# Token-factor normalisations of six operations at other places of a mixture-of-experts kernel on one core

## The chip, the cores and the metric

One Trainium2 chip, one of its cores. The metric is the device time of one execution in microseconds (us). Shown are the median of three runs and one execution that the profiler recorded. The engines are called as the profile calls them: PE is TensorE, DVE is VectorE, ACT is ScalarE, POOL is GpSimd, SP issues the DMAs.

## The reference, cut to what matters

The program runs an mLSTM attention, a dense feed-forward layer, and a mixture of eight experts whose token factors are normalised over rows and columns eight times. Only the last part bears on the change:

```python
logits = x @ w_gate                        # x: 1536 x 320, w_gate: 320 x 8
logits = logits - logits.max()
P = np.exp(logits)
for _ in range(8):
    P /= P.sum(1, keepdims=True) + 1e-09   # rows: over the 8 experts
    P /= P.sum(0, keepdims=True) + 1e-09   # columns: over the 1536 tokens
    P *= N / E
for e in range(E):                         # F = 1024
    ye = np.maximum(x @ w1[e], 0.0) @ w2[e]
    out += P[:, e:e + 1] * ye
```

## The kernel before

All products are made of fp32r matmuls on values split into a high and a low part. After attention and the dense layer comes `tc.manual_schedule()`: from there each engine works through its instructions in the order in which the Python code emits them, and the order is written by hand.

The work of the experts is cut into units of 256 hidden columns: four units for each of eight experts, `experts[0]` to `experts[31]`, and two halves of 768 tokens, `q` = 0 and 1. `order` lists the 64 pairs: units 0, 1, 2 for q = 0, then the same for q = 1, then unit 3 for both, then one unit after the other for both halves. For the i-th pair, `up_c(i)` computes the hidden values by seven products of four matmuls each (`product`, lines 835 to 838), accumulated in four PSUM banks `b0` to `b3`: a fast matrix multiplication, which needs seven sums of pieces of the input (`X`, in 7 slices of 3 parts) and of the weights. Around them ACT copies the first product to `s0`; DVE adds it into `s1`, `s2` and into `c11`, `c10`, `c01` (lines 863, 866, 854), which frees banks 3, 2 and 3 again; ACT makes `hh` (rounded, line 855) and a full-precision copy (856) of each, POOL the low part `hl` (857). `hh00` and `hl00` come straight from bank 0 by ACT and DVE (872, 873). `down_c(i)` computes six outputs `y` of 128 tokens, six matmuls each (lines 172 to 174), in three PSUM banks in turn: the fourth output needs the bank of the first, so it needs the first to have been taken out. For the first unit (n = 0) an output is copied into `acc` (by ACT if it is odd, line 902, by DVE if it is even, line 904), for the others it is added by DVE (906 or 908). The loop calls `up_c(i + 1)`, then `down_c(i)`.

Everything else is hung into slots: `when(g, slot, fn)` has `fn` emitted at slot 0 to 6 behind the seven products of `up_c(g + 1)`, or at slot 7 to 12 behind the six outputs of `down_c(g)`. What is called **group g** here is that stretch, `up_c(g + 1)` and `down_c(g)`; group -1 is `up_c(0)`. Each function issues to several engines at once, and on each its instructions stand behind what was emitted there before. In the slots are:

- for q = 1, three positions (each two blocks of 128 tokens) that become `X[1]`: `repeat` (POOL copies), `turn` (4 PE transposes into the one bank of pool `ps_s`, and an ACT copy `rawE` or `rawx`, line 251), `sums` (two DVE subtractions for each k, line 257), `high` (an ACT conversion of 4 or 3 slices, line 222), `low` (DVE, 225), `rest` (POOL, 229);
- the gate: `logits` (matmuls, line 757), `logits_turn` to `exps`, which find the maximum and the exponentials `Pg`, 128 x 12 x 8; then eight times `rows` (798 to 801), `columns` (a matmul by ones into `cps`, 805) and `columns_end` (808 to 811);
- `scale_first` (918), which scales the accumulators of expert 0 by `Pg` before those of expert 1 are added;
- loading, `sums`, `split1` and `split2` of the next units' weights (ACT 213 and 222; POOL 214, 201, 225, 229).

Of the kernel before, what the change touches and what calls it, by code (L numbers as in the profile page):

```python
# [38 lines left out]
def mlstm_moe_kernel(ctx, tc, qp, q3, kp, kn, vn, gates_in, og, cst_in, scr_in, w_in, w_out, w_gate, w1, w2, out):  # L39
# [703 lines left out]
    nc.gpsimd.memset(ones, 1.0)  # L743
    Pg = cp.tile([P, NCK, E], F32, tag="Pg", name="Pg")
# [44 lines left out]
    def top_all():  # L789
        gate_state['mps'] = ps_s.tile([P, 512], F32, tag="b1", name="mps2")  # L790
        nc.tensor.matmul(gate_state['mps'][:, 0:1], ones[0:1, :], gate_state['m1'][:, 0:1], start=True, stop=True)
# [5 lines left out]
    def rows():  # L797
        nc.vector.tensor_reduce(out=rs, in_=Pg, axis=AX.X, op=ALU.add)
        nc.vector.tensor_scalar(out=rs, in0=rs, scalar1=1e-9, scalar2=None, op0=ALU.add)
# [3 lines left out]
    def columns(it):  # L803
        gate_state['cps'] = ps_s.tile([P, NCK, E], F32, tag="b1", name=f"cps{it}")
        nc.tensor.matmul(gate_state['cps'], ones, Pg, start=True, stop=True)

    def columns_end():
        nc.vector.tensor_reduce(out=cs, in_=gate_state['cps'].rearrange("p t e -> p e t"), axis=AX.X, op=ALU.add)
        nc.vector.tensor_scalar(out=cs, in0=cs, scalar1=1e-9, scalar2=None, op0=ALU.add)
        nc.vector.reciprocal(cs, cs)  # L810
        nc.vector.scalar_tensor_tensor(out=Pg, in0=Pg, scalar=float(NT / E), in1=cs.unsqueeze(1).to_broadcast([P, NCK, E]),
                                       op0=ALU.mult, op1=ALU.mult)
# [72 lines left out]
    def down_c(i):  # L885
# [6 lines left out]
        for b in range(2):  # L892
            for p in range(HP):
# [7 lines left out]
                if n == 0 and t % 2:  # L901
                    nc.scalar.activation(o, y, AF.Copy)
                elif n == 0:
                    nc.vector.tensor_copy(o, y)  # L904
# [27 lines left out]
    for g, s, p, k in ((-1, 2, 1, 0), (-1, 4, 1, 1), (0, 0, 2, 0), (0, 3, 2, 1)):  # L932
        when(g, s, x1[p].turn, k, ps_s, rawE if p == 1 else None)
    for p, times in enumerate((((-1, 0), (-1, 1), (-1, 3), (-1, 4)), ((0, 1), (0, 2), (0, 4), (0, 5)), ((0, 8), (0, 9), (0, 11), (1, 0)))):
        for k in range(2):
            if p:
                when(*((-1, 5), (-1, 6), (0, 6), (0, 7))[2 * p - 2 + k], x1[p].sums, V, k)
            when(*times[k], x1[p].high, k)
            when(*times[2 + k], x1[p].low, k, V)
            when(*times[2 + k], x1[p].rest, k, GP)  # L940

    for g, s, q, i in ((1, 4, 0, 0), (1, 7, 0, 1), (1, 9, 1, 0), (1, 12, 1, 1)):
# [146 lines left out]
```

## Time and profile before

| | |
|---|---|
| median of 3 runs | 983.21 us (982.13 to 984.79) |
| the profiled execution | 981.5 us, its span 979.8 us |
| PE busy | 944.1 us, 96% of the span |
| DVE, ACT, POOL busy | 60%, 51%, 62% |
| mean granted clock of PE | 0.974 |

The experts take the span from 296 us on. In the timelines a row gives the start, the duration, engine and line, output and input tiles, shapes and the number of merged instructions; brackets at the end hold the engine's idle time before it and what released it. PE's matmuls are pipelined, so successive rows overlap: what counts is the distance of their starts. In the view of stretches the granted clock is a share of full speed: 1.00 is 2.4 GHz, 0.50 is 1.2 GHz.

### The profile page before, as it was taken

Reading aid. Unit: us, or ns where it says so; the run is one execution under the profiler, and the core shown is the slowest. Engines: PE = TensorE matmul, PEld = TensorE weight load, DVE = VectorE, ACT = ScalarE, POOL = GpSimd, SP = SyncE. Lnnn points to the kernel's source line nnn. Section 1 sums busy time; section 2 is a strip of 40 time slices with the busy share of each in tenths; the row PEclk is TensorE's granted clock in tenths of the full one; section 3 lists DMA queues with packets and bytes.
Section 4 is the critical chain, followed back from the end, with each engine's and each line's share of the span. In section 5 each row is a group of like instructions: output and inputs, shape, how many; then the busy total and the mean of one; then the engine's idle time right before and its main releaser. Section 6 shows DMA issues by size and latency. Waiting matters only on the chain.

```text
span 979.8 us, 16868 instructions
## 1 busy us (share of the span) xinstructions
PE 944.1 (96%) x6174; PEld 918.3 (94%) x6174; DVE 583.5 (60%) x1137; ACT 496.0 (51%) x969; POOL 606.2 (62%) x615
## 2 busy tenths in 40 slices
PE   7699999999998988999999999999999999999998
PEld 5588998999997888999999999999999999999998
DVE  5977524152566568666666656666566665666655
ACT  5757544534656343654554545445454454544542
POOL 3552634533475455577677777777777777777762
PEclk7779999999999999999999999999999999999999
DMA  7644321011110100111111111111111111111102
GB/s 254 205 156 134 107 72 60 29 53 39 30 56 21 36 19 28 33 50 49 36 36 43 49 50 36 36 44 49 49 36 36 44 49 49 36 36 44 41 1 81
DMA packets 57160, 56.63 MB, mean 58 GB/s; under 512 B 7558, under 2 KB 47670, under 8 KB 57078
## 3 DMA queue, kind: packets, MB, share of 16 engines
q1 hardware_dynamic: 57078, 55.56, 18.7%
q8 instruction: 48, 0.79, 0.3%
q14 instruction: 34, 0.28, 0.1%
HBM read 53.57 MB, written 1.97 MB: 57 GB/s over the span
## 4 chain that ended last, share of the span: by engine, by line
PE 85%; DVE 7%; ACT 3%; issue 2%; POOL 1%; DMA 1%; SPq 1%; DVEq 0%; ACTq 0%; POOLq 0%
PE y L172 11%; PE y L173 11%; PE y L174 11%; PE b L835 8%; PE b L838 8%; PE b L836 8%; PE b L837 7%; PE ha L165 7%; PE ya L172 2%; PE ya L174 2%; PE ya L173 2%; PE yps L471 2%; PE sps L457 1%; PE zps L475 1%; DVE c L854 1%
## 5 line engine op out<-in xcount | busy, mean ns | idle before, releaser
L857 POOL TENSOR_TENSOR hl<-c,hh 128x384 fp32r<-128x384 f32 x192 | 196.8, 1025 | 185.2 <-ACT c L856 160.1
L172 PE MATMUL y<-w_e,hh 128*128 128x320 f32 x768 | 237.7, 310 | 3.0 <-DVE acc L904 1.7
L173 PE MATMUL y<-w_e,hh 128*128 128x320 f32 x768 | 236.3, 308 | 0.0
L174 PE MATMUL y<-w_e,hl 128*128 128x320 f32 x768 | 236.0, 307 | 0.0
L908 DVE SCALAR_TENSOR_TENSOR acc<-y,Pg,acc 128x320 f32<-128x320 f32 x336 | 179.4, 548 | 63.3 <-PE y L174 56.1
L855 ACT ACTIVATE hh<-c 128x384 fp32r<-128x384 f32 x192 | 99.9, 520 | 218.0 <-DVE c L854 218.0
L835 PE MATMUL b<-X,w_e 128*128 128x384 f32 x448 | 152.9, 341 | 1.4 <-DVE c L854 1.4
L836 PE MATMUL b<-X,w_e 128*128 128x384 f32 x448 | 151.6, 338 | 0.0
L838 PE MATMUL b<-X,w_e 96*128 96x384 f32 x448 | 151.5, 338 | 0.0
L837 PE MATMUL b<-X,w_e 128*128 128x384 f32 x448 | 151.0, 337 | 0.0
L172 PEld LDWEIGHTS y<-w_e,hh 128*128 128x128 f32 x768 | 144.1, 188 | 4.8 <-DVE acc L904 2.4
L173 PEld LDWEIGHTS y<-w_e,hh 128*128 128x128 f32 x768 | 144.0, 188 | 0.0
L174 PEld LDWEIGHTS y<-w_e,hl 128*128 128x128 f32 x768 | 144.0, 187 | 0.0
L544 POOL TENSOR_TENSOR hla<-gg,hha 128x256 fp32r<-128x256 f32 x90 | 72.6, 810 | 95.9 <-ACT hha L543 84.4
L165 PE MATMUL ha<-xT,w_a 128*128 128x256 f32 x768 | 111.1, 288 | 0.9 <-ACT xT L282 0.6
L856 ACT ACTIVATE c<-c 128x384 f32<-128x384 f32 x192 | 100.9, 525 | 17.8 <-ACT hh L855 0.7
L854 DVE TENSOR_TENSOR c<-b,s 128x384 f32<-128x384 f32 x192 | 100.8, 552 | 11.8 <-PE b L838 4.5
L165 PEld LDWEIGHTS ha<-xT,w_a 128*128 128x128 f32 x768 | 101.9, 193 | 5.3 <-issue 2.2
L873 DVE SCALAR_TENSOR_TENSOR hl<-b,hh 128x384 fp32r<-128x384 f32 x64 | 35.7, 558 | 102.2 <-ACT hh L872 102.2
L201 POOL TENSOR_TENSOR raw_e<-raw_e 128x256 f32<-128x256 f32 x116 | 84.4, 738 | 4.5
L835 PEld LDWEIGHTS b<-X,w_e 128*128 128x128 f32 x448 | 85.0, 190 | 2.2 <-DVE c L854 1.7
L836 PEld LDWEIGHTS b<-X,w_e 128*128 128x128 f32 x448 | 85.2, 190 | 0.0
(164 smaller groups left out, 1547.6 us busy)
## 6 DMA issues: line engine op xcount, KB each, us to landing
raw_e<-in_w_dram SPq DMA_DIRECT2D x32, 320.0 KB, 2.9
raw_e<-in_w_dram SPq DMA_DIRECT2D x62, 128.0 KB, 2.2
raw_e<-in_w_dram SPq DMA_DIRECT2D x248, 32.0 KB, 1.8
raw_a<-in_w_in_dram SPq DMA_DIRECT2D x8, 768.0 KB, 4.3
raw_a<-in_w_out_dram SPq DMA_DIRECT2D x8, 640.0 KB, 3.9
R<-in_kp_dram SPq DMA_DIRECT2D x11, 256.0 KB, 2.9
R<-in_qp_dram SPq DMA_DIRECT2D x11, 256.0 KB, 3.0
R<-in_vn_dram SPq DMA_DIRECT2D x11, 184.5 KB, 2.5
```

The costliest lines, as they stand in the source:

```text
L165: nc.tensor.matmul(h_ps, t1[:, ws, c * P:(c + 1) * P], xt[:, xs, t0:t0 + n], start=(j == 0), stop=(j == len(MM1) - 1),)
L172: nc.tensor.matmul(y_ps, a, t2[:, c, :], start=first, stop=False)
L173: nc.tensor.matmul(y_ps, a, t2[:, 2 + c, :], start=False, stop=False)
L174: nc.tensor.matmul(y_ps, b, t2[:, c, :], start=False, stop=last)
L835: nc.tensor.matmul(bank, f[:, 0], b[:, 0], start=fresh, stop=False, skip_group_check=not fresh)
L836: nc.tensor.matmul(bank, f[:, 0], b[:, 2], start=False, stop=False, skip_group_check=not fresh)
L837: nc.tensor.matmul(bank, f[:, 2], b[:, 0], start=False, stop=False, skip_group_check=not fresh)
L838: nc.tensor.matmul(bank, f[0:K3, 1], b[0:K3, 1], start=False, stop=True, skip_group_check=not fresh)
L854: nc.vector.tensor_tensor(c, part, plus, op=ALU.add)
L856: nc.scalar.activation(c, c, AF.Relu)
L857: nc.gpsimd.tensor_tensor(hl[a][b], c, hh[a][b].bitcast(F32), op=ALU.subtract)
L908: nc.vector.scalar_tensor_tensor(out=o, in0=y, scalar=Pg[:, 2 * HP * q + t, e:e + 1], in1=o, op0=ALU.mult, op1=ALU.add)
```

## The change

- `Pg` becomes a view of a tile `Pgx` of 13 x 9: a ninth column and a thirteenth block hold constants (1e-9, and 1e-9 / 128), so that the row sums and the column sums already contain the 1e-9. The factor N / E goes into the ones of the column matmul, by E / N. `rows` and `columns_end` have three DVE operations each instead of four.
- All six outputs of the first unit are copied by ACT.
- Slots: the sums of position 1 for q = 1 stand one and four slots later, its `high`, `low`, `rest` some four slots later; position 2's `turn` one and two slots later, its sums three, its conversions in group 1. The conversion `split2` of unit 1 goes from group -1 to group 0. The logits of q = 1 go from group 1 to group 2, the gate's steps follow into groups 2 and 3. `columns` stay at slots 2 and 8, the first at slot 8 of group 3 instead of slot 2; `columns_end` now stands at slots 3 and 9 (before 4 and 10), `rows` at 3 and 11 (before 4 and 10). `scale_first` comes one group later.

```diff
@@ -740,8 +740,14 @@
     ps_u = ctx.enter_context(tc.tile_pool(name="ps_u", bufs=1, space=PSUM))
 
     ones = cp.tile([P, P], F32, tag="ones", name="ones")
-    nc.gpsimd.memset(ones, 1.0)
-    Pg = cp.tile([P, NCK, E], F32, tag="Pg", name="Pg")
+    nc.gpsimd.memset(ones, float(E / NT))
+    one = cp.tile([1, P], F32, tag="one", name="one")
+    nc.gpsimd.memset(one, 1.0)
+
+    Pgx = cp.tile([P, NCK + 1, E + 1], F32, tag="Pg", name="Pg")
+    nc.gpsimd.memset(Pgx[:, 0:NCK], 1e-9)
+    nc.gpsimd.memset(Pgx[:, NCK], 1e-9 / P)
+    Pg = Pgx[:, 0:NCK, 0:E]
     rs = cp.tile([P, NCK], F32, tag="rs", name="rs")
     cs = cp.tile([P, E], F32, tag="cs", name="cs")
     nmx = cp.tile([P, 1], F32, tag="nmx", name="nmx")
@@ -788,28 +794,26 @@
 
     def top_all():
         gate_state['mps'] = ps_s.tile([P, 512], F32, tag="b1", name="mps2")
-        nc.tensor.matmul(gate_state['mps'][:, 0:1], ones[0:1, :], gate_state['m1'][:, 0:1], start=True, stop=True)
+        nc.tensor.matmul(gate_state['mps'][:, 0:1], one, gate_state['m1'][:, 0:1], start=True, stop=True)
 
     def exps():
         nc.vector.tensor_copy(nmx, gate_state['mps'][:, 0:1])
         nc.scalar.activation(Pg, Pg, AF.Exp, bias=nmx)
 
     def rows():
-        nc.vector.tensor_reduce(out=rs, in_=Pg, axis=AX.X, op=ALU.add)
-        nc.vector.tensor_scalar(out=rs, in0=rs, scalar1=1e-9, scalar2=None, op0=ALU.add)
+        nc.vector.tensor_reduce(out=rs, in_=Pgx[:, 0:NCK], axis=AX.X, op=ALU.add)
         nc.vector.reciprocal(rs, rs)
         nc.vector.tensor_tensor(Pg, Pg, rs.unsqueeze(2).to_broadcast([P, NCK, E]), op=ALU.mult)
 
     def columns(it):
-        gate_state['cps'] = ps_s.tile([P, NCK, E], F32, tag="b1", name=f"cps{it}")
-        nc.tensor.matmul(gate_state['cps'], ones, Pg, start=True, stop=True)
+        gate_state['cps'] = ps_s.tile([P, NCK + 1, E], F32, tag="b1", name=f"cps{it}")
+        nc.tensor.matmul(gate_state['cps'], ones, Pgx[:, :, 0:E], start=True, stop=True)
 
     def columns_end():
+
         nc.vector.tensor_reduce(out=cs, in_=gate_state['cps'].rearrange("p t e -> p e t"), axis=AX.X, op=ALU.add)
-        nc.vector.tensor_scalar(out=cs, in0=cs, scalar1=1e-9, scalar2=None, op0=ALU.add)
         nc.vector.reciprocal(cs, cs)
-        nc.vector.scalar_tensor_tensor(out=Pg, in0=Pg, scalar=float(NT / E), in1=cs.unsqueeze(1).to_broadcast([P, NCK, E]),
-                                       op0=ALU.mult, op1=ALU.mult)
+        nc.vector.tensor_tensor(Pg, Pg, cs.unsqueeze(1).to_broadcast([P, NCK, E]), op=ALU.mult)
 
 
 
@@ -898,10 +902,8 @@
                 for a in range(2):
                     mm2(y, hh[a][b], hl[a][b], p, u.w2, a, a == 0, a == 1)
                 o = acc[q][:, t]
-                if n == 0 and t % 2:
+                if n == 0:
                     nc.scalar.activation(o, y, AF.Copy)
-                elif n == 0:
-                    nc.vector.tensor_copy(o, y)
                 elif e == 0:
                     nc.vector.tensor_tensor(o, y, o, op=ALU.add)
                 else:
@@ -929,31 +931,35 @@
 
     for p in (1, 2):
         when(-1, (0, 2)[p - 1], x1[p].repeat, copy_rest)
-    for g, s, p, k in ((-1, 2, 1, 0), (-1, 4, 1, 1), (0, 0, 2, 0), (0, 3, 2, 1)):
+    for g, s, p, k in ((-1, 2, 1, 0), (-1, 4, 1, 1), (0, 1, 2, 0), (0, 5, 2, 1)):
         when(g, s, x1[p].turn, k, ps_s, rawE if p == 1 else None)
-    for p, times in enumerate((((-1, 0), (-1, 1), (-1, 3), (-1, 4)), ((0, 1), (0, 2), (0, 4), (0, 5)), ((0, 8), (0, 9), (0, 11), (1, 0)))):
+
+    for p, sums, highs, lows, rests in ((0, None, ((-1, 0), (-1, 1)), ((-1, 3), (-1, 4)), ((-1, 3), (-1, 4))),
+                                        (1, ((-1, 6), (0, 3)), ((0, 5), (0, 6)), ((0, 7), (0, 8)), ((0, 7), (0, 9))),
+                                        (2, ((0, 9), (0, 10)), ((1, 4), (1, 5)), ((1, 8), (1, 10)), ((1, 6), (1, 8)))):
         for k in range(2):
             if p:
-                when(*((-1, 5), (-1, 6), (0, 6), (0, 7))[2 * p - 2 + k], x1[p].sums, V, k)
-            when(*times[k], x1[p].high, k)
-            when(*times[2 + k], x1[p].low, k, V)
-            when(*times[2 + k], x1[p].rest, k, GP)
-
-    for g, s, q, i in ((1, 4, 0, 0), (1, 7, 0, 1), (1, 9, 1, 0), (1, 12, 1, 1)):
+                when(*sums[k], x1[p].sums, V, k)
+            when(*highs[k], x1[p].high, k)
+            when(*lows[k], x1[p].low, k, V)
+            when(*rests[k], x1[p].rest, k, GP)
+
+    for g, s, q, i in ((1, 4, 0, 0), (1, 7, 0, 1), (2, 1, 1, 0), (2, 5, 1, 1)):
         when(g, s, logits, q, i)
-    for s, fn in ((0, logits_turn), (2, logits_sum), (4, top_turn), (6, top_one), (8, top_all), (9, exps), (11, rows)):
-        when(2, s, fn)
+    for g, s, fn in ((2, 8, logits_turn), (2, 9, logits_sum), (2, 11, top_turn), (2, 12, top_one), (3, 1, top_all), (3, 2, exps),
+                     (3, 7, rows)):
+        when(g, s, fn)
+
     for it in range(8):
-        g, s = 3 + it // 2, 6 * (it % 2)
-        when(g, s + 2, columns, it)
-        when(g, s + 4, columns_end)
-        if it < 7:
-            when(g, s + 4, rows)
+        g = 3 + (it + 1) // 2
+        for s, fn in zip(((8, 9, 11), (2, 3, 3))[it % 2], (lambda it=it: columns(it), columns_end, rows)):
+            if it < 7 or fn is not rows:
+                when(g, s, fn)
     for q in range(2):
         for t in range(2 * HP):
-            when(7 + q, (0, 0, 1, 1, 2, 2)[t], scale_first, q, t)
-
-    when(-1, 6, experts[1].split2, GP)
+            when(8 + q, (0, 0, 1, 1, 2, 2)[t], scale_first, q, t)
+
+    when(0, 4, experts[1].split2, GP)
     when(0, 12, experts[2].split2, GP)
     for n in range(3, NU):
         u, g = experts[n], 2 * n - 4
```

On DVE around the second unit's products (`up_c(1)`, group 0; `c10_0` and `c01_0` belong to the unit before, `rawE` is position 1 of q = 1). Before:

```order
L854 TENSOR_TENSOR c10_0_3418<-b2_0_3347,s1_0_3358 128x384
L257 TENSOR_TENSOR rawE_3344<-rawE_3344 128x256 x2
L854 TENSOR_TENSOR c01_0_3429<-b3_0_3348,s1_0_3358 128x384
L257 TENSOR_TENSOR rawE_3344<-rawE_3344 128x256 x2
L863 TENSOR_TENSOR s1_1_3452<-b1_1_3440,s0_1_3451 128x384
L866 TENSOR_TENSOR s2_1_3453<-b2_1_3441,s1_1_3452 128x384
L854 TENSOR_TENSOR c11_1_3482<-b3_1_3442,s2_1_3453 128x384
```

and now:

```order
L858 TENSOR_TENSOR c10_0_3422<-b2_0_3351,s1_0_3362 128x384
L858 TENSOR_TENSOR c01_0_3431<-b3_0_3352,s1_0_3362 128x384
L257 TENSOR_TENSOR rawE_3348<-rawE_3348 128x256 x2
L867 TENSOR_TENSOR s1_1_3451<-b1_1_3439,s0_1_3450 128x384
L870 TENSOR_TENSOR s2_1_3452<-b2_1_3440,s1_1_3451 128x384
L858 TENSOR_TENSOR c11_1_3479<-b3_1_3441,s2_1_3452 128x384
L257 TENSOR_TENSOR rawE_3348<-rawE_3348 128x256 x2
```

`c01_0` has passed the first pair of sums, and the second pair has gone behind `c11_1`.

On ACT in group 0, from `hh00` of the second unit to the outputs of the first (`y0_0` to `y0_5`; `X1` is `X[1]`, `rawE` position 1, `rawx_1_2` position 2). Before:

```order
L872 ACTIVATE hh00_1_3443<-b0_1_3439 128x384
L855 ACTIVATE hh10_1_3445<-c10_1_3505 128x384
L856 ACTIVATE c10_1_3505<-c10_1_3505 128x384
L855 ACTIVATE hh01_1_3444<-c01_1_3516 128x384
L856 ACTIVATE c01_1_3516<-c01_1_3516 128x384
L902 ACTIVATE acc0_3342<-y0_1_3533 128x320
L222 ACTIVATE X1_3343<-rawx_1_2_3459 128x4x2x128
L222 ACTIVATE X1_3343<-rawx_1_2_3459 128x3x2x128
L902 ACTIVATE acc0_3342<-y0_3_3551 128x320
```

and now:

```order
L876 ACTIVATE hh00_1_3442<-b0_1_3438 128x384
L213 ACTIVATE w2_e0_1_3492<-raw2_e0_1_3289 128x640
L859 ACTIVATE hh10_1_3444<-c10_1_3499 128x384
L860 ACTIVATE c10_1_3499<-c10_1_3499 128x384
L251 ACTIVATE rawx_1_2_3463<-px1_1_2_3504 128x4x128
L222 ACTIVATE X1_3347<-rawE_3348 128x4x2x128
L859 ACTIVATE hh01_1_3443<-c01_1_3515 128x384
L860 ACTIVATE c01_1_3515<-c01_1_3515 128x384
L222 ACTIVATE X1_3347<-rawE_3348 128x3x2x128
L906 ACTIVATE acc0_3346<-y0_0_3521 128x320
L906 ACTIVATE acc0_3346<-y0_1_3531 128x320
```

The conversion of `w2`, one copy and both conversions into `X1` of position 1 now stand between `hh00` and the first output's copy; before, that copy was DVE's, and the conversions of position 1 stood ahead of `hh11`.

On DVE in group 4, from `c11` of `up_c(5)` to the next `c`. Before:

```order
L854 TENSOR_TENSOR c11_5_4093<-b3_5_4044,s2_5_4055 128x384
L873 SCALAR_TENSOR_TENSOR hl00_5_4049<-b0_5_4041,hh00_5_4045 128x384
L808 TENSOR_REDUCE cs_3340<-cps2_4086 128x8
L809 TENSOR_SCALAR cs_3340<-cs_3340 128x8
L810 RECIPROCAL cs_3340<-cs_3340 128x8
L811 SCALAR_TENSOR_TENSOR Pg_3338<-Pg_3338,cs_3340 128x96
L798 TENSOR_REDUCE rs_3339<-Pg_3338 128x12
L799 TENSOR_SCALAR rs_3339<-rs_3339 128x12
L800 RECIPROCAL rs_3339<-rs_3339 128x12
L801 TENSOR_TENSOR Pg_3338<-Pg_3338,rs_3339 128x96
L854 TENSOR_TENSOR c10_5_4118<-b2_5_4043,s1_5_4054 128x384
```

and now:

```order
L858 TENSOR_TENSOR c11_5_4084<-b3_5_4035,s2_5_4046 128x384
L814 TENSOR_REDUCE cs_3344<-cps1_4077 128x8
L815 RECIPROCAL cs_3344<-cs_3344 128x8
L816 TENSOR_TENSOR Pg_3340<-Pg_3340,cs_3344 128x12x8
L804 TENSOR_REDUCE rs_3343<-Pg_3340 128x12
L805 RECIPROCAL rs_3343<-rs_3343 128x12
L806 TENSOR_TENSOR Pg_3340<-Pg_3340,rs_3343 128x12x8
L877 SCALAR_TENSOR_TENSOR hl00_5_4040<-b0_5_4032,hh00_5_4036 128x384
L858 TENSOR_TENSOR c10_5_4107<-b2_5_4034,s1_5_4045 128x384
```

The normalisation, two operations shorter, has passed `hl00`.

## Rows read from the trace of the kernel before

**Rows 1.** The page, busy time, share and instructions of each engine.

```profile
PE 944.1 (96%) x6174; PEld 918.3 (94%) x6174; DVE 583.5 (60%) x1137; ACT 496.0 (51%) x969; POOL 606.2 (62%) x615
```

**Rows 2.** Waits of PE: line waiting, line waited for, total us, times, longest.

```profile
PE cps L805 <- DVE Pg L801: 5.6, 5, 2.0
...
PE y L172 <- DVE acc L904: 1.7, 2, 1.4
PE px L250 <- ACT rawx L251: 1.6, 1, 1.6
...
PE b L835 <- DVE c L854: 1.4, 1, 1.4
PE y L172 <- ACT acc L902: 1.2, 1, 1.2
...
PE mps L791 <- DVE m L786: 0.2, 1, 0.2
```

**Rows 3.** Timeline of PE: starts of groups, and places at which it waited.

```profile
316.72 0.41 PE L172 MATMUL y<-w_e,hh 128*128 128x320 f32 x1 [1.44 <-DVE acc L904]
...
320.01 0.34 PE L835 MATMUL b<-X,w_e 128*128 128x384 f32 x1
...
361.45 0.34 PE L835 MATMUL b<-X,w_e 128*128 128x384 f32 x1
...
363.56 0.36 PE L805 MATMUL cps<-Pg,ones 128*128 128x96 f32 x2
...
363.96 0.34 PE L836 MATMUL b<-X,w_e 128*128 128x384 f32 x1
...
374.46 0.34 PE L835 MATMUL b<-X,w_e 128*128 128x384 f32 x1
...
440.61 0.34 PE L835 MATMUL b<-X,w_e 128*128 128x384 f32 x1
...
450.81 0.34 PE L835 MATMUL b<-X,w_e 128*128 128x384 f32 x1
```

**Rows 4.** Timeline of DVE in group 0 and group 3.

```profile
303.18 2.18 DVE L257 TENSOR_TENSOR rawE<-rawE 128x256 f32<-128x256 f32 x2
...
309.33 0.56 DVE L854 TENSOR_TENSOR c<-b,s 128x384 f32<-128x384 f32 x1
...
351.15 0.56 DVE L854 TENSOR_TENSOR c<-b,s 128x384 f32<-128x384 f32 x1 [0.40 <-PE b L838]
353.29 0.56 DVE L873 SCALAR_TENSOR_TENSOR hl<-b,hh 128x384 fp32r<-128x384 f32 x1 [1.59 <-ACT hh L872]
353.77 0.25 DVE L808 TENSOR_REDUCE cs<-cps 128x8 f32<-128x96 f32 x1
...
355.55 0.26 DVE L801 TENSOR_TENSOR Pg<-Pg,rs 128x96 f32<-128x96 f32 x1
...
360.88 0.87 DVE L801 TENSOR_TENSOR Pg<-Pg,rs 128x96 f32<-128x96 f32 x1
```

**Rows 5.** Timeline of ACT in group 0.

```profile
305.86 0.53 ACT L855 ACTIVATE hh<-c 128x384 fp32r<-128x384 f32 x1 [1.49 <-DVE c L854]
...
306.85 0.72 ACT L213 ACTIVATE w_e<-raw_e 128x640 fp32r<-128x640 f32 x1
...
310.98 0.58 ACT L251 ACTIVATE rawx<-px 128x512 f32<-128x512 f32 x1
...
316.64 0.42 ACT L902 ACTIVATE acc<-y 128x320 f32<-128x320 f32 x1
316.96 1.05 ACT L222 ACTIVATE X<-rawx 128x1024 fp32r<-128x1024 f32 x1
```

**Rows 6.** Timeline of POOL beside the last row of rows 4.

```profile
360.63 1.00 POOL L229 TENSOR_TENSOR w_e<-raw_e,w_e 32x384 fp32r<-32x384 f32 x1
```

**Rows 7.** Stretches: from:to, length, PE, PEld, DVE, ACT, POOL busy (instructions), granted clock, DMA share, GB/s.

```profile
308.00:312.00 4.00, 3.52 (x14) 3.52 (x15) 1.68 (x4) 3.90 (x7) 2.38 (x3) 0.57 0.18 49
12.00:38.00 26.00, 18.31 (x87) 16.31 (x88) 22.28 (x38) 17.71 (x27) 13.23 (x10) 0.50 0.68 232
```

## The prediction

> **What bounds the kernel now.** First the busy line of the page: TensorE (PE) is busy 944 of 979.8 us [rows 1], so only two things can shorten the kernel: less matmul work, which the change doesn't offer, or fewer places where PE waits. Next the waits of PE, longest first: of those in the stretch that the change touches, the column sums `cps` wait five times for VectorE (DVE), 5.6 us in all, and four further kinds of wait hold 1.7, 1.6, 1.4 and 1.2 us, and one more 0.2 [rows 2]. The reader should see there that all of them name DVE or ScalarE (ACT) as the late one, although both are busy little over half the span: it is a matter of where things stand in their queues. Last the timelines, for what a wait costs. A group without normalisation takes 450.81 - 440.61 = 10.20 us [rows 3]. The group from 361.45 to 374.46 takes 13.01, which is 2.81 more. It holds two `cps`; one that doesn't wait puts 363.96 - 363.56 = 0.40 between matmuls that stand 0.175 apart in a clean group, so 0.23 each [rows 3]; the one that waits idles 2.0 [rows 2]. The 0.36 left over is what PE loses in stopping and starting again: 0.4 for each wait.
>
> Why `cps` waits is in DVE's rows: behind `c11` (351.15) DVE idles 1.59 us until ACT has delivered `hh00` (353.29), and only then come the eight small operations of a normalisation, 353.77 to 355.81 [rows 4]. They stand behind a gap and not in it.
>
> **The change, part by part.**
>
> *Normalisations.* Eight operations become six: four of them reduce or take a reciprocal, two multiply. At 0.25 to 0.29 from start to start that is 1.6 us, and they now stand directly behind `c11`, in the gap of 1.59: `hl00` starts as before, and everything behind it 2.04 us earlier. The other half (one column sum behind the third output, the row sums behind the fifth) has over 2 us before the next `cps`, since three products of 0.7 stand between. So the five waits go: 5.6 + 5 x 0.4 = 7.6. The wait of the maximum goes too, for its matmul now stands behind two products of the next group: 0.2 + 0.4 = 0.6. What is late next: the first row sums still stand behind `c01` in group 3, and the first `cps` two outputs later; three operations (0.8) and two `c` (1.0) behind `hl00` instead of eight (2.04) leave about 0.8 of a wait of 1.0, with the restart 1.2.
>
> *A rule against this part.* A multiply of Pg by its row factors takes 0.26 us alone and 0.87 while GpSimd (POOL) runs a weight operation of 1.00 [rows 4, 6]: it ends only when POOL's does. In group 5 POOL converts weights just where the six operations now stand, so I charge 0.6 once. The Trainium skill (SBUF — State Buffer, Who interferes with whom) says that a VectorE instruction with two SBUF inputs shares a read path with GpSimd and is held until the other's whole instruction is over, and that a reduction never is. By that rule both multiplies may be held, in each group in which POOL is busy; it is the third rival below. The multiply now skips every ninth element; contiguous and free it is 0.26, held 0.87, and I take 0.26 for the rest.
>
> *Output copies on ACT.* In group 3 the wait for an ACT copy, 1.2 + 0.4, mostly goes: the row sums no longer hold `c01` back, and ACT gets its inputs earlier; but six copies of 0.42 [rows 5] now stand in one queue with a weight conversion between the first and second, and I leave 0.35.
>
> So groups 2 to 6 give 7.6 + 0.6 + 1.6 - 1.2 - 0.6 - 0.35 = 7.65 us.
>
> *The first unit's outputs (group 0).* Before, `c01` of the first product stood behind two sums that took 2.18 (303.18) [rows 4]; ACT idled 1.49 for it (305.86), then converted `w2` for 0.72 (306.85), and only then made the `s` for which the next product's chain waits [rows 5]. Now `c01` comes first and the conversion later: `s`, the two sums behind it and `c11` come about 2.1 earlier, `c11` at 307.2 instead of 309.33 [rows 4]. From there a chain runs to the copy that frees a bank for the fourth output: `c11` 0.56, three ACT operations 1.6, `hl00` and `c10` 1.2, two ACT operations 1.15, then `rawx` (0.5), the two conversions into X (0.95 and 0.75 in a row; the larger takes 1.05 by itself at 316.96 [rows 5]), `hh01` and its copy 1.0 between them, and the copy of the first output 0.42: 8.1 us, which ends at 315.3. DVE no longer takes this copy, and it stands behind the conversions, while before the same distance was 316.72 - 309.33 = 7.4 [rows 3, 4]. So the fourth output starts 1.4 earlier. The wait of 0.3 behind it (1.7 less 1.4 [rows 2]) and its restart go as well: the next unit, before at 320.01 [rows 3], starts 2.1 earlier.
>
> PE itself will be there far sooner. The waits of 1.4 and 1.6 shrink to some 0.6 and 0.5, and the low clock after them goes, so it stands before the fourth output at about 311.8 and waits 3.5 us in one piece. Two pieces of 1.4 and 1.6 took the granted clock to 0.57 over 308 to 312, that is mostly to 1.2 GHz; PE was busy 3.52 us there, which cost 3.52 x 0.43 = 1.5 [rows 2, 7]. I take it that one piece of 3.5 does the same: 2.1 - 1.5 = 0.6. Bounds: 2.1 if it doesn't, nothing if the spell is half as long again.
>
> *Costed at nothing.* The sixteen small additions taken out of DVE (it isn't on the path outside the waits above). Three memsets on POOL, ahead of copies that PE needs only at its fourth product. The column sums' 104 columns for 96, by 0.175 for 384 some 4 ns a pass. Two products of gate logits that go from group 1 to group 2: the same PE time, one group later. The scaling of the accumulators one group later, under the same ACT idle time. The last third of X, made in group 1 instead of group 0: it is due at group 2's first two products. Its two POOL pieces (about 2.3) follow the last `hl` of group 1, which by the same steps as above ends some 4.4 into the outputs: 6.7. The outputs take 10.20 - 7 x 0.7 = 5.3 and logits of 9 x 0.175 = 1.6 between them, the first product 0.7 more: 7.6. That leaves 0.9; without this cover see the fourth rival.
>
> **The sum.** 7.65 + 0.6 = 8.25 us. The profiled execution took 981.5 and would take 973.2; the median of the runs shown is 983.21, 1.7 higher, and against it the forecast is **975.0**.
>
> **Rivals.**
> 1. The clock stays up in group 0: 2.1 instead of 0.6, **973.5**. For it: single waits of 2.0 in the normalisations left it up. Against: 3.5 in one piece is more than the 3.0 in two that didn't. Chance 0.20.
> 2. Slower: one fall of the clock doesn't end. Its place is group 0 to group 3, where the long wait, the shorter ones around it and the first `cps` follow each other. In the kernel's beginning, with such stop and go, the granted clock is 0.50 from 12 to 38 us [rows 7]. Each us at that level loses half a us, so the 9.75 us that the change gives without a fall are used up by a spell of 19.5; from 25.4 us on the kernel is slower by over 0.3% (2.95 us, about what a measurement can tell from no change). As long as the 26 of the beginning: 983.2 - 9.75 + 13 = **986.5**. Against: before, the same stretch recovers within 4 us. Chance 0.02.
> 3. Both multiplies are held by POOL, in groups 4 and 5: 1.6 + 2 x 1.0 in a gap of 1.59, `hl00` 2.0 late, outputs wait 2.0 + 0.4 in each, less the 0.6 charged: **979.2**. For it: 0.87 in the row quoted. Against: before, such an operation was held in only a few of the groups. Chance 0.15.
> 4. X is late for group 2: one POOL piece of 1.0 and a DVE piece of 0.6 behind it, and a restart: 2.0 more, less some of the cover, **976.7**. Chance 0.10.
>
> **The numbers.** The forecast's own case has 0.45, and 0.08 is left for sizes that I got wrong in other ways. Range 971.5 to 979.5: below, the clock stays up and the 2.15 us of waits left over are nothing; above, the third rival. Faster by more than 2.95 us are all cases but the second and a sum of the third and fourth with more: 0.93; within it 0.05; slower 0.02.
>
> **What would show it.** In the profile after: `cps` waits once or hardly at all, where it waited five times; behind `c11` the six operations fill the gap, and `hl00` starts some 2.1 behind `c11`; groups 4 and 6 take 10.7 to 10.9 us. The waits of PE name an ACT copy in group 0 with 3 to 4 us, and the granted clock drops behind it. I am wrong if `cps` still waits for DVE in groups 4 to 6, if the fourth output of the first unit starts no earlier against the start of that unit, or if group 2's first products wait for X.

## The result, and the profile after

The changed kernel takes 973.75 us (median of 4 runs, 971.02 to 975.78) against 983.28 of the kernel before in the same series: a ratio of 0.9893, 95% interval 0.9849 to 0.9937. The forecast was 975.0. The profiled execution is the fastest of the four, 971.02 us with a span of 969.1. The page, busy line (it answers to [rows 1]):

```profile
PE 941.9 (97%) x6174; PEld 917.8 (95%) x6174; DVE 574.9 (59%) x1115; ACT 498.3 (51%) x975; POOL 609.1 (63%) x618
```

The waits of PE in the stretch that the change touches (against [rows 2]):

```profile
PE y L172 <- ACT acc L906: 3.2, 1, 3.2
...
PE cps L810 <- DVE Pg L806: 0.6, 1, 0.6
...
PE b L839 <- ACT s L864: 0.5, 1, 0.5
PE b L839 <- DVE s L870: 0.3, 1, 0.3
```

Eleven waits with 11.7 us in all have become four with 4.6. `cps` waits once where it waited five times, and the largest that is left is the copy of the first output by ACT.

PE's timeline, the same places as in [rows 3]: the fourth output of group 0, the first product of the next unit, group 4 with a `cps` that doesn't wait, and the start of group 5:

```profile
313.71 0.64 PE L172 MATMUL y<-w_e,hh 128*128 128x320 f32 x1 [3.18 <-ACT acc L906]
...
317.75 0.34 PE L839 MATMUL b<-X,w_e 128*128 128x384 f32 x1
...
356.83 0.34 PE L839 MATMUL b<-X,w_e 128*128 128x384 f32 x1
...
358.95 0.36 PE L810 MATMUL cps<-Pg,ones 128*128 128x104 f32 x2
359.09 0.43 PE L839 MATMUL b<-X,w_e 128*128 128x384 f32 x1
...
367.51 0.34 PE L839 MATMUL b<-X,w_e 128*128 128x384 f32 x1
```

Group 4 takes 367.51 - 356.83 = 10.68 where it took 13.01. DVE's timeline in that group shows why (against [rows 4]):

```profile
360.14 0.56 DVE L858 TENSOR_TENSOR c<-b,s 128x384 f32<-128x384 f32 x1 [0.41 <-PE b L842]
360.62 0.26 DVE L814 TENSOR_REDUCE cs<-cps 128x8 f32<-128x104 f32 x1
...
361.14 0.26 DVE L816 TENSOR_TENSOR Pg<-Pg,cs 128x96 f32<-128x96 f32 x1
...
362.00 0.26 DVE L806 TENSOR_TENSOR Pg<-Pg,rs 128x96 f32<-128x96 f32 x1
362.29 0.56 DVE L877 SCALAR_TENSOR_TENSOR hl<-b,hh 128x384 fp32r<-128x384 f32 x1
362.76 0.55 DVE L858 TENSOR_TENSOR c<-b,s 128x384 f32<-128x384 f32 x1
```

`hl00` starts 2.15 behind `c11` (before: 353.29 - 351.15 = 2.14), now with the whole normalisation done. The next `c` starts 0.47 behind `hl00`, and no small operation stands between.

In group 0 the second unit's `c11` starts at 305.86, which is 11.06 behind the first product of the first unit (294.80). Before, it was 309.33 - 296.04 = 13.29. DVE:

```profile
305.86 0.56 DVE L858 TENSOR_TENSOR c<-b,s 128x384 f32<-128x384 f32 x1
```

ACT then copies the first three outputs in one go behind its last conversion into `X`:

```profile
312.51 0.83 ACT L222 ACTIVATE X<-rawE 128x768 fp32r<-128x768 f32 x1
313.24 1.07 ACT L906 ACTIVATE acc<-y 128x320 f32<-128x320 f32 x3
```

PE waits 3.18 for it, which is called the hole in what follows, and behind the hole the granted clock is down (columns as in [rows 7]):

```profile
310.50:313.70 3.20, 0.02 (x1) 0.00 (x0) 1.03 (x2) 3.11 (x7) 1.74 (x2) 0.92 0.31 84
313.70:318.00 4.30, 4.29 (x20) 4.29 (x21) 3.77 (x5) 1.53 (x5) 2.62 (x2) 0.66 0.23 63
```

At 0.66 the 4.29 us of work lose 4.29 x 0.34 = 1.46.

**Where the time went, by group.** The first product of each `up_c` has its own row in PE's timeline; the distances of these starts are the lengths of the groups, and they repeat from execution to execution to some 0.05 us, except where the clock falls. From the first product of the first unit to that of the tenth:

| kernel | -1, 0 | 1 | 2 | 3 | 4 to 6 | 7 | sum |
|---|---|---|---|---|---|---|---|
| before | 23.97 | 15.47 | 12.38 | 13.59 | 38.24 | 10.24 | 113.89 |
| after | 22.95 | 12.81 | 14.00 | 12.27 | 32.42 | 10.41 | 104.86 |
| norm_only | 23.98 | 15.43 | 11.35 | 13.03 | 32.42 | 10.41 | 106.62 |
| place_undone | 23.87 | 13.26 | 14.00 | 12.27 | 35.41 | 10.85 | 109.66 |
| eight_ops | 23.00 | 12.81 | 13.96 | 12.23 | 35.10 | 10.80 | 107.90 |
| extra_recip | 23.19 | 12.81 | 13.99 | 12.26 | 33.61 | 10.42 | 106.28 |
| fill | 21.68 | 12.79 | 14.00 | 12.26 | 32.42 | 10.40 | 103.55 |
| sums_undone | 23.26 | 12.80 | 14.01 | 12.26 | 32.43 | 10.41 | 105.17 |
| copies_undone | 20.77 | 14.41 | 13.99 | 14.57 | 32.43 | 10.41 | 106.58 |
| copies_again | 20.78 | 14.43 | 14.00 | 14.58 | 32.43 | 10.42 | 106.64 |
| dve_copies | 18.20 | 13.85 | 14.22 | 12.26 | 32.42 | 10.41 | 101.36 |
| best | 18.22 | 12.81 | 14.77 | 12.28 | 32.42 | 10.42 | 100.92 |
| best2 | 18.20 | 12.80 | 14.80 | 11.06 | 32.41 | 10.42 | 99.69 |
| after_again | 23.19 | 12.81 | 14.00 | 12.27 | 32.42 | 10.41 | 105.10 |

The change gains 113.89 - 104.86 = 9.03 here (groups 1 and 2 exchange the logits of q = 1 and are read together). The span became 10.7 shorter; 1.24 of that lies ahead of the first unit, which started at 294.80 instead of 296.04. That stretch holds none of the moved work and scatters: in the fourteen profiled executions the first unit starts between 294.47 and 299.66, while what lies behind the start of the tenth unit differs by 0.83 at most (by 0.44 between before and after). So in what follows the lengths of groups decide, from one profiled execution of each kernel, and totals stand beside them; the 95% intervals of several totals overlap that of the changed kernel.

### The profile page after: what moved, and what is told of

Same layout as the page of the kernel before. It is cut to its first block, busy times and chain, and to the rows that moved or that the text cites. A ratio compares the mean times of both kernels' runs of the same rounds, so it can differ in the third digit from the quotient of the medians.

```text
span 969.1 us, 16853 instructions
## 1 busy us (share of the span) xinstructions
PE 941.9 (97%) x6174; PEld 917.8 (95%) x6174; DVE 574.9 (59%) x1115; ACT 498.3 (51%) x975; POOL 609.1 (63%) x618
## 4 chain that ended last, share of the span: by engine, by line
PE 89%; DVE 4%; ACT 2%; issue 1%; POOL 1%; DMA 1%; SPq 1%; DVEq 0%; ACTq 0%; POOLq 0%
PE y L172 12%; PE y L173 12%; PE y L174 12%; PE b L839 8%; PE b L840 8%; PE b L842 8%; PE b L841 8%; PE ha L165 8%; PE ya L172 2%; PE ya L174 2%; PE ya L173 2%; PE yps L471 2%; PE sps L457 1%; PE zps L475 1%; DMA qP_c<-in_qp_dram 1%
```

## The experiments

**The normalisation alone (norm_only).** The diff of the change as far as `Pgx`, `ones`, the gate's slots and `scale_first`; everything else as before.

> The normalisation's edit alone; front slots, output copies and logits of q = 1 as before. Theory 1 (the place in DVE's gap makes the gain): groups -1 to 1 stay at 39.4 us, group 2 takes 11.4 (12.4 before), groups 3 to 6 take 44.7 (51.8 before, 44.7 with the whole change), and the total is 8 us below before: 975.3. Rival (the moves in front and the copies on ACT make a large part of it, because ACT and DVE enter group 3 less late): groups 3 to 6 take over 47, the total is less than 6 us below before: above 977.

Measured: 976.11 us (ratio to before 0.9936, 0.9907 to 0.9964). Groups -1 to 1 and 2 came as theory 1 said, groups 3 to 6 took 45.45 instead of 44.7, and the total lies between the two expectations. The edit alone gives 113.89 - 106.62 = 7.3 of the 9.03. The 0.76 that group 3 misses is a wait of the first `cps`; DVE's timeline ahead of it:

```profile
357.57 0.48 DVE L908 COPY acc<-y 128x320 f32<-128x320 f32 x1
357.96 0.25 DVE L804 TENSOR_REDUCE rs<-Pg 128x12 f32<-128x108 f32 x1
...
358.51 1.04 DVE L806 TENSOR_TENSOR Pg<-Pg,rs 128x96 f32<-128x96 f32 x1
```

A DVE copy of an output stands ahead of the row sums, and their multiply is stretched from 0.26 to 1.04; `cps` waits 1.8 for it, 0.6 with the whole change. So the moves of copies bear on group 3 too.

**Place against number.** Two kernels, each with one half of the change to the normalisation. Place_undone keeps six operations:

```diff
-        for s, fn in zip(((8, 9, 11), (2, 3, 3))[it % 2], ...
+        for s, fn in zip(((8, 10, 10), (2, 4, 4))[it % 2], ...
```

> The changed kernel with six operations in each normalisation, but at the old slots 4 and 10, so that they stand behind hl00 again. Theory 1 (place): cps waits come back in groups 4, 5 and 6, each some 0.45 shorter than the 1.0 to 2.0 of before since two operations are gone, and each costs a restart of 0.4: about 1.0 a group, groups 4 to 6 take 35.4 (32.4 with the whole change, 38.2 before), the total is 3 us above the changed kernel: 976.7. Rival (number of operations): groups 4 to 6 stay within 0.5 of 32.4, the total within 1 us of 973.75.

Eight_ops keeps the new slots and takes `rows`, `columns`, `columns_end` and their tiles from the kernel before.

> The changed kernel with eight operations in each normalisation, as before, at the new slots, in the gap. Theory 1 (place): they take 2.04 in a gap of 1.59, hl00 comes 0.45 later, and since a hl00 that came 0.8 late in group 5 of the changed kernel cost nothing, this costs nothing either: groups 4 to 6 take 32.4 to 32.9, the total is 0 to 1 us above the changed kernel, 974.2. Rival (number of operations): a wait of 0.45 and a restart of 0.4 in each group, groups 4 to 6 take 35, the total is 976.5 or more.

Measured: 977.38 us (0.9943, 0.9917 to 0.9969) and 978.69 us (0.9957, 0.994 to 0.9973). Groups 4 to 6 took 35.41 and 35.10. Place_undone did what theory 1 said, to 0.01. Eight_ops did what the rival said. Of the 5.82 us between 38.24 and 32.42, fewer operations at the old place give 38.24 - 35.41 = 2.83, and the new place with the old operations gives 38.24 - 35.10 = 3.14: number and place are worth about the same. In place_undone `cps` waits in each group; PE's timeline:

```profile
367.87 0.44 PE L810 MATMUL cps<-Pg,ones 128*128 128x104 f32 x2 [0.92 <-DVE Pg L806]
...
379.55 0.44 PE L810 MATMUL cps<-Pg,ones 128*128 128x104 f32 x2 [0.64 <-DVE Pg L806]
```

In eight_ops the operations are in the gap, but they take far longer than 2.04. DVE in group 5, and POOL beside it:

```profile
375.04 0.56 DVE L854 TENSOR_TENSOR c<-b,s 128x384 f32<-128x384 f32 x1 [0.27 <-PE b L838]
375.52 0.25 DVE L808 TENSOR_REDUCE cs<-cps 128x8 f32<-128x96 f32 x1
375.80 1.06 DVE L809 TENSOR_SCALAR cs<-cs 128x8 f32<-128x8 f32 x1
...
377.13 0.91 DVE L811 SCALAR_TENSOR_TENSOR Pg<-Pg,cs 128x96 f32<-128x96 f32 x1
...
379.01 0.55 DVE L873 SCALAR_TENSOR_TENSOR hl<-b,hh 128x384 fp32r<-128x384 f32 x1
```
```profile
375.55 1.29 POOL L229 TENSOR_TENSOR w_e<-raw_e,w_e 32x512 fp32r<-32x512 f32 x1
376.91 1.02 POOL L857 TENSOR_TENSOR hl<-c,hh 128x384 fp32r<-128x384 f32 x1
```

The addition of 1e-9 takes 1.06 and ends at 376.86, POOL's instruction at 376.84; the multiply ends at 378.04, POOL's next at 377.93. `hl00` comes 3.97 behind `c11`, and the outputs wait. So both are held, that is, stretched until POOL's instruction ends. The two removed operations are worth more here than their own 0.45: they are additions of a constant, and POOL holds one of them as it holds the multiply.

**Eight operations that aren't held (extra_recip).** To split own time from holding:

```diff
         nc.vector.tensor_reduce(out=rs, in_=Pgx[:, 0:NCK], axis=AX.X, op=ALU.add)
+        nc.vector.reciprocal(rs2, rs)
...
+        nc.vector.reciprocal(cs2, cs)
```

> The changed kernel with a fourth operation added to rows and to columns_end: a reciprocal into a tile that nobody reads, so eight operations stand in the gap as in the run with eight operations, but of the two added ones none was seen stretched beside GpSimd (reciprocals take 0.20 to 0.23 in every row, while the additions and multiplications with a scalar that they replace took 0.17 to 1.06). Theory 2 (eight operations cost through those that GpSimd holds): hl00 comes 0.45 to 0.5 later, too little to cost anything, groups 4 to 6 take 32.4 to 33.2 (32.42 with six operations, 35.10 with the old eight). Rival (eight operations are too many by their own time): groups 4 to 6 take 34.5 or more.

Measured: 974.9 us (0.9918, 0.9896 to 0.994), groups 4 to 6 33.61: group 4 11.63, group 5 10.92, group 6 11.06, against 10.68, 10.88 and 10.86 with six. The sum lies between both expectations, 0.4 above theory 2's upper end; the groups tell why. DVE, `c11` and `hl00` of groups 4 and 5, with the two multiplies of group 4 and the longer one of group 5:

```profile
363.47 0.56 DVE L862 TENSOR_TENSOR c<-b,s 128x384 f32<-128x384 f32 x1 [0.41 <-PE b L846]
...
364.71 0.80 DVE L820 TENSOR_TENSOR Pg<-Pg,cs 128x96 f32<-128x96 f32 x1
...
366.37 0.83 DVE L809 TENSOR_TENSOR Pg<-Pg,rs 128x96 f32<-128x96 f32 x1
367.12 0.55 DVE L881 SCALAR_TENSOR_TENSOR hl<-b,hh 128x384 fp32r<-128x384 f32 x1
...
375.09 0.56 DVE L862 TENSOR_TENSOR c<-b,s 128x384 f32<-128x384 f32 x1 [0.22 <-PE b L846]
...
376.33 0.67 DVE L820 TENSOR_TENSOR Pg<-Pg,cs 128x96 f32<-128x96 f32 x1
...
378.03 0.55 DVE L881 SCALAR_TENSOR_TENSOR hl<-b,hh 128x384 fp32r<-128x384 f32 x1
```

In group 4 both multiplies are held (0.80 and 0.83 for 0.26), `hl00` comes 3.65 behind `c11`, and the group loses 0.95: a `hl00` 1.5 late costs 1. Eight_ops takes as long there (11.64), so this group doesn't tell the kinds of operation apart. In group 5 `hl00` comes 2.94 behind `c11`, but with six operations it comes 2.92 behind (373.72 - 370.80 in the rows of the next section), since its multiplies are held for longer there (0.90 and 0.50). In group 6 it comes no later either, and the 0.20 that the group loses lie ahead of its `c11`. So the `hl00` 0.45 late, on which theory 2 rested, came in no group, and what 0.45 of own time alone costs is not shown. Shown is that with the same number of operations groups 5 and 6 are shorter by 1.03 and 0.46 than in eight_ops (11.94 and 11.52): of the 2.7 that eight_ops lost, 1.5 go with the kind of operation. The other 1.2 come with the number, most of them in group 4, where two more operations shift how the multiplies fall against POOL.

**The hole and the clock (fill).**

```diff
+    def fill():
+        t = ps_s.tile([P, 512], F32, tag="b1", name="fill")
+        for _ in range(16):
+            nc.tensor.matmul(t[:, 0:NQ], experts[0].factor(0)[:, 0], X[0][:, 0, 0], ...)
+    when(0, 9, fill)
```

> The changed kernel with 16 matmuls of 128 x 384 behind the third output of group 0, into a bank that nobody reads: PE works in the hole of 3.2 us and waits no less for the copy. Theory 1 (the hole makes the low clock): granted clock 1.00 from 304 to 320, and from the fourth output (313.7 in the changed kernel) to the first product of the next unit 2.6 us instead of 4.05; groups -1 and 0 take 21.5 instead of 22.95. Rival (the clock falls for another reason, such as the load of the other engines or the waits before the hole): a granted clock of 0.5 to 0.8 behind the hole as before, 22.95 or more.

Measured: 970.22 us (0.9866, 0.984 to 0.9893). Groups -1 and 0 take 21.68, and the granted clock stays up; the stretches over the hole and behind it, columns as in [rows 7]:

```profile
312.20:315.20 3.00, 3.00 (x17) 2.71 (x17) 1.05 (x2) 2.91 (x6) 1.51 (x2) 1.00 0.32 90
315.20:318.00 2.80, 2.80 (x20) 2.80 (x20) 2.77 (x3) 1.46 (x4) 2.64 (x2) 1.00 0.35 96
```

Theory 1 holds: the fourth output starts as late as without the added matmuls (18.93 and 18.91 behind the first unit's start), but PE works meanwhile, the clock stays up, and groups -1 and 0 get back 1.3 to 1.5 (against after and after_again).

**The sums alone moved back (sums_undone).**

```diff
-                                        (1, ((-1, 6), (0, 3)), ...
+                                        (1, ((-1, 5), (-1, 6)), ...
```

> The changed kernel with the sums of position 1 back at the slots of before, ahead of c01 and of the next unit's sums. Theory 1 (the 2.1 us by which the chain to the first copy came earlier are these sums): c11 of the second unit comes 2 us later than in the changed kernel, measured from the first product of the first unit (11.06 there), the wait of 1.4 of that unit's last product comes back, and the copy of the first output ends 1.5 to 2 us later; groups -1 and 0 take 24.5 to 25 (22.95 in the changed kernel, 23.97 before). Rival (the conversions on ACT set the copy's time, whatever DVE does): the copy ends within 0.5 of where it did, groups -1 and 0 take 23 to 23.5.

Measured: 973.57 us (0.99, 0.9872 to 0.9928). `c11` comes 12.66 behind the first unit's start instead of 11.06, the wait of 1.36 is back, and the copies start 20.04 behind that start instead of 18.44: the parts of theory 1 hold with 1.6 of the 2.23 by which `c11` came earlier; the rest, which would fit the later conversion of `w2`, was not tested. But groups -1 and 0 take 23.26, the length that the rival gave though not by its mechanism: 0.31 more than in one execution of the changed kernel and 0.07 more than in the other. The stretches, from the waits ahead of the hole (307.3) over the hole (314.5) to the next unit, show why:

```profile
307.30:311.00 3.70, 3.50 (x13) 3.00 (x14) 1.94 (x4) 2.18 (x5) 1.27 (x2) 0.59 0.00 0
311.00:314.50 3.50, 3.50 (x23) 3.31 (x21) 1.42 (x4) 2.95 (x6) 2.95 (x3) 0.94 0.10 29
314.50:316.40 1.90, 0.08 (x1) 0.00 (x0) 0.83 (x2) 1.81 (x5) 1.00 (x1) 1.00 0.33 87
316.40:319.20 2.80, 2.77 (x19) 2.77 (x20) 2.77 (x3) 1.51 (x4) 2.64 (x2) 1.00 0.36 98
```

It falls earlier, behind waits of 1.36, 0.53 and 0.20, and PE works slowly in time that it would otherwise have waited: the hole is 1.85, and the clock doesn't fall behind it. From the fourth output to the next unit this kernel takes 2.75, as fill does (the changed kernel 4.04): so what fill got back is the low clock, and not the stop before it. The move of the sums by itself brought 0.1 to 0.3: what it gave in time, the hole took back as a low clock.

**The copies alone moved back (copies_undone, and once more as copies_again).** The kernel with the two lines of before for `n == 0`.

> The changed kernel with the even outputs of the first unit copied by DVE again, as before. Theory 1 (the hole is ACT's queue, not the choice of the copy's engine alone): the first copy no longer waits, but the second still stands behind the conversions on ACT, so the hole moves from the fourth output to the fifth and shrinks from 3.2 to 2.3; groups -1 and 0 take 22.0 (22.95), group 3 takes 13.0 as in the run of the normalisation alone (12.27), the total stays within 1 us of 973.75. Rival (the even copies alone make the hole): no wait over 1 us at the outputs of group 0, groups -1 and 0 take 19.5 or less.

> The kernel with the even outputs copied by DVE a second time. In its first profile the granted clock fell to 0.50 behind a wait of 1.82 of the first cps in group 3 and made that group 14.57 long; in the run of the normalisation alone the same wait stood at the same place and the clock stayed at 1.00 (13.03). Theory 1 (the same wait lets the clock fall in one execution and not in another): the wait of 1.8 is there again, group 3 takes 13.0 or 14.6, whichever, groups -1 and 0 take 20.8 or some 1.5 more if the clock falls behind the hole of 2.3, and the total scatters by 1.5 and more around 976. Rival (the clock's course is the program's): group 3 takes 14.57 and groups -1 and 0 take 20.77 again, to 0.1.

Measured: 976.06 us (0.9912, 0.9887 to 0.9937) and 973.4 (0.989, 0.9868 to 0.9912); by groups both are alike to 0.1. The hole went where theory 1 put it; PE's timeline at the fifth output:

```profile
316.56 0.41 PE L172 MATMUL y<-w_e,hh 128*128 128x320 f32 x1 [2.31 <-ACT acc L906]
```

but the clock stayed at 1.00 behind it, so groups -1 and 0 take 20.8 and not 22.0. The gain is given back: in group 1, 1.6 (a wait of 1.01 of the logits for ACT, which runs late because the last copy by DVE, and behind it the next unit's additions, stand behind 4.4 us of position 2's sums), and in group 3, 2.3 (`cps` waits 1.8 as in norm_only, and here the clock falls), in the stretches of copies_undone, columns as in [rows 7]:

```profile
358.00:360.00 2.00, 2.00 (x9) 2.00 (x8) 0.97 (x4) 0.44 (x1) 0.92 (x1) 0.50 0.00 1
```

The rival of the second run was right: the fall in group 3 repeats. By groups the copies on ACT are worth 1.5 to 1.8 us in sum (106.58 and 106.64 against 105.10 and 104.86): 3.9 in groups 1 and 3, less 2.2 to 2.4 that they cost in group 0. But 1.5 of it is the low clock in group 3 (14.57 and 14.58, where norm_only takes 13.03 with the same wait); without that fall neither choice would be clearly better. Of the two totals one shows it and the other doesn't.

**A better version, in three steps.** First (dve_copies) the copies for q = 0 all on DVE, with nothing long ahead of them:

```diff
-                if n == 0:
+                if n == 0 and q:
                     nc.scalar.activation(o, y, AF.Copy)
+                elif n == 0:
+                    nc.vector.tensor_copy(o, y)
...
-    (1, ((-1, 6), (0, 3)), ((0, 5), (0, 6)), ((0, 7), (0, 8)), ((0, 7), (0, 9))),
-    (2, ((0, 9), (0, 10)), ((1, 4), (1, 5)), ((1, 8), (1, 10)), ((1, 6), (1, 8)))
+    (1, ((-1, 6), (0, 3)), ((0, 5), (0, 6)), ((0, 9), (0, 11)), ((0, 7), (0, 9))),
+    (2, ((1, 3), (1, 3)), ((1, 4), (1, 5)), ((1, 8), (1, 10)), ((1, 6), (1, 8)))
```

> The changed kernel with the first unit's outputs for q = 0 all copied by DVE instead of ACT, the low parts of position 1 two slots later and the sums of position 2 behind c11 of the next unit, so that the copies stand behind nothing long on DVE. Theory 1 (the hole of 3.2 us before the fourth output is the first copy's place behind conversions on ACT, and the low clock after it follows from the hole): hole gone, granted clock 1.00 from 304 to 320, groups -1 and 0 take 18.5 us (22.95 with the whole change), the total is 4.5 below the changed kernel: 969.3. Rival 1 (the low clock comes without the hole): 1.5 us less of that, 970.8. Rival 2 (the next unit waits for DVE instead, whose sums and low parts stand behind the copies): less than 2 us below, 972 or more.

Measured: 969.75 us (0.9876, 0.985 to 0.9902). Groups -1 and 0 take 18.20: hole and low clock are gone, 4.75 us, as theory 1 said. Group 1 gives 1.0 back, by a wait of 0.85 of the logits behind a conversion on ACT. The second step (best): `rows` of group 3 from slot 7 to 3, the first logits from slot 4 to 3.

> The kernel with the copies for q = 0 on DVE, and two more moves: the first rows in the gap behind c11 of group 3 instead of behind its c01, and the first logits one product earlier, ahead of a conversion on ACT that kept lT from leaving the bank. Theory 1: the wait of 0.6 of the first cps with its restart of 0.4 goes, and the wait of 0.9 of the logits with 0.4; group 1 takes 12.6 (13.85), group 3 11.3 (12.26), the total is 2.2 below that kernel's 969.75: 967.5. Rival (the time is given back at what is late next, hh00 behind lT in group 1 or hl00 behind the row sums in group 3): less than 1 us below.

Measured: 969.5 us (0.9874, 0.9851 to 0.9896). The 2.2 did not come. Group 1 is 1.04 shorter, as said; group 2 took 0.55 of it back (its first two products wait for parts of `X` from POOL, the first for 0.24), and group 3 gained nothing. The wait of `cps` went, and another stood behind it, at the fourth output in PE's timeline:

```profile
352.15 0.41 PE L172 MATMUL y<-w_e,hh 128*128 128x320 f32 x1 [0.87 <-ACT acc L906]
```

The third step (best2), `if n == 0 and q and t > 1`, gives the first two copies of q = 1 to DVE.

> The kernel before it in the series (copies for q = 0 on DVE, first rows in the gap, logits one product earlier) with the first two outputs for q = 1 copied by DVE too. Theory 1 (in group 3 two late ones stood behind each other: the first row sums, whose going uncovered a wait of 0.87 for the first copy on ACT): that wait and its restart of 0.4 go, group 3 takes 11.0 to 11.3 (12.28), first product of the first unit to the first of the tenth 99.7 (100.92; 104.86 with the whole change), the total is 1.2 lower. Rival (a third wait stands behind the second, such as the column sums behind the two copies on DVE): group 3 stays over 12.

Measured: 967.81 us (0.9841, 0.982 to 0.9862), group 3 11.06. Of the waits of PE in this stretch three are left, the largest 0.5. In the same series the changed kernel was timed again:

> The changed kernel itself, in the same series as its improvement, so that the two are timed on one chip. Theory 1: groups -1 to 8 take 104.9 to 106.3 by the length of the low clock behind the hole (22.95 and 24.3 were seen for groups -1 and 0 with the same program up to there), the total 973.75 within 1.5. Rival (the first timing was a lucky one): above 976.

Measured: 974.58 us (0.9899, 0.9882 to 0.9916). The intervals don't touch: best2 is faster than both kernels, 5.4 us by groups (105.10 - 99.69) and 6.8 by the medians.

## Why the prediction was right, point by point

- **The five waits, 7.6.** Right in kind and size. The four of groups 4 to 6 go; that of group 3 shrinks from 1.03 to 0.64. The step "six operations fill the gap" was right, but the gain is place and number in about equal parts: eight operations don't only overshoot by 0.45, they also put more in POOL's way. With the small additions left in (eight_ops), 2.7 of the gain is lost; the prediction costed them at nothing outside the waits. In groups 4 to 6 the four waits were 5.6 - 1.03 = 4.6 with four restarts of 0.4, 6.2; measured 5.82.
- **The charge of 0.6 for a multiply held by POOL.** It was held, in group 5 and in group 6, where I had expected it once. DVE and POOL of the changed kernel:

```profile
370.80 0.56 DVE L858 TENSOR_TENSOR c<-b,s 128x384 f32<-128x384 f32 x1 [0.40 <-PE b L842]
...
371.80 0.90 DVE L816 TENSOR_TENSOR Pg<-Pg,cs 128x96 f32<-128x96 f32 x1
...
373.30 0.50 DVE L806 TENSOR_TENSOR Pg<-Pg,rs 128x96 f32<-128x96 f32 x1
373.72 0.55 DVE L877 SCALAR_TENSOR_TENSOR hl<-b,hh 128x384 fp32r<-128x384 f32 x1
...
383.56 1.10 DVE L806 TENSOR_TENSOR Pg<-Pg,rs 128x96 f32<-128x96 f32 x1
```
```profile
371.30 1.29 POOL L229 TENSOR_TENSOR w_e<-raw_e,w_e 32x512 fp32r<-32x512 f32 x1
```

  `hl00` came 2.92 and 2.87 behind `c11` instead of 2.15, and that cost 0.2 in each group (10.88 and 10.86 against 10.68): it has slack that the prediction didn't count. The rule of the Trainium skill (SBUF — State Buffer, Who interferes with whom), that an instruction of DVE with two SBUF inputs is held until POOL's instruction is over and a reduction never is, agrees with this trace: 371.80 + 0.90 = 372.70, POOL's end is 372.59, and no reduction here is over 0.27. No reciprocal is over 0.23.
- **What is left in group 3: 1.2 and 0.35.** The first `cps` waits 0.64 where 0.8 was worked out, and no output waits there; best2, in which neither it nor the ACT copy waits, shows both together at 12.27 - 11.06 = 1.21. The 0.35 is no second term: best shows that the two waits overlap, and one hides the other.
- **Group 0, 0.6.** The profile shows 1.02, the second one 0.78. `c11` came 2.23 earlier (2.1 predicted), the fourth output 1.77 (1.4), the hole was 3.2 (3.5), the low clock cost 1.46 (1.5). The mis-sized term is mostly the chain from `c11` to the end of the first copy, 7.8 instead of 8.1. That the hole makes the low clock, on which rival 1 hung, is shown by fill.
- **The gate's steps in groups 1 and 2, 0.6.** They gave 27.85 - 26.81 = 1.04; norm_only has the same 1.07, so it is the steps' moving and not the logits'. The maximum's matmul is part of it, which now counts in group 3: 346.37 - 345.79 = 0.58 lie between the matmuls around it there, 0.40 more than between two in a row. And a second stop went, which the prediction left out: before, the maximum's transpose started 340.29 - 339.85 = 0.44 behind the matmul ahead of it, now 343.57 - 343.42 = 0.15.
- **The rivals.** No spell without end. Both multiplies held in one group, rival 3, came in group 5 of the changed kernel (0.90 and 0.50) without its price; the price, about 1 a group, is shown by group 4 of extra_recip, where `hl00` comes 3.65 behind `c11`. Against it the prediction said that before such an operation was held in only a few of the groups; the trace of before shows a multiply held (0.51 to 0.87) and an addition held (0.54 to 0.75) in each of groups 3 to 6. X was not late for group 2; in best, where it is done 1.85 behind the start of that group instead of 0.46, it is, by 0.24 (rival 4's mechanism).

By groups the sum was 8.25 and came to 9.03: 1.02 for 0.6 in groups -1 and 0, 1.04 for 0.6 in groups 1 and 2, 1.32 for 1.45 in group 3 (1.4 + 1.6 - 1.2 - 0.35), 5.82 for 5.6 in groups 4 to 6 (6.2 - 0.6), and -0.17 for nothing in group 7, into which the last `cps` moved. Of the 10.7 between the two profiled executions, 1.24 was scatter ahead of the change.

## What to carry to other kernels

Put small work on an engine into a gap where it waits for another engine anyway, and count not only its own time but which of its operations a neighbour can hold: here replacing an addition by a constant already in the data removed more than its 0.2 in the groups in which POOL would have held it. When a copy is moved to another engine, read what stands ahead of it in that queue: here the copies were better on ACT in two groups and worse in the one in which ACT was converting, and choosing per half, with DVE's long sums out of their way, beat both. A wait that goes may uncover one behind it, so look at the next late one before the gain is counted twice.

## What was not expected of the hardware

- The granted clock fell to 0.50 (1.2 GHz) behind the hole of 3.2 in all five profiled executions with it, and not behind one of 2.31 in either run of copies_undone. It did fall behind one of 1.82 in group 3 of those two runs, and not behind the same wait at the same place in norm_only, nor behind one of 1.96 in group 4 of before. What decides between them stays open.
- A low clock isn't always a loss: in sums_undone it lay in time that PE would have waited. And its cost varies with the same program: place_undone, which is the changed kernel up to group 3, took 0.92 more in groups -1 and 0 and 0.45 more in group 1, with the clock low for longer, as its stretch from 318 on shows (columns as in [rows 7]):

```profile
318.00:322.00 4.00, 4.00 (x17) 4.00 (x16) 1.14 (x3) 1.82 (x4) 0.26 (x2) 0.59 0.00 1
```

- POOL holds an addition of a constant too (1.06 for 0.17 in eight_ops), though it has one tensor as its input. The trace of before already shows it; DVE and POOL in its group 6, with ends at 388.30 and 388.27:

```profile
387.62 0.68 DVE L799 TENSOR_SCALAR rs<-rs 128x12 f32<-128x12 f32 x1
```
```profile
387.26 1.01 POOL L229 TENSOR_TENSOR w_e<-raw_e,w_e 32x384 fp32r<-32x384 f32 x1
```
